# Row sums of ten attention heads with one more addition and half the columns, in a score buffer

## The chip, the cores and the metric

The program runs on one core of a Trainium2 chip. The metric is the time of one execution on the device, in microseconds (us). The engines are TensorE (PE in the rows, its weight loads PEld), VectorE (DVE), ScalarE (ACT), GpSimd (POOL) and SyncE (SP, which issues DMAs).

## What is computed

Clustered attention over 2 x 8 heads of 768 tokens with 64 dimensions, then a mixture of experts with a capacity of 384 rows. The change touches the row sums of the softmax alone (`np.sum(attn, ...)`).

```python
mask = q_assign[:, :, :, None] == k_assign[:, :, None, :]
scores = np.where(mask, scale * np.matmul(q, k.transpose(0, 1, 3, 2)), -1000000000.0)
attn = np.exp(scores - np.max(scores, axis=-1, keepdims=True))
attn = attn / (np.sum(attn, axis=-1, keepdims=True) + 1e-09)
attn_out = np.matmul(attn, v)
...
logits = x @ w_gate                     # x: attn_out, one row a token
h = np.maximum(np.einsum('ecd,edf->ecf', disp, w1), 0.0)
y = np.einsum('ecf,efd->ecd', h, w2)
out[i] = gate_w[i] * y[expert_idx[i], pos[i]]
```

## The kernel before

The 16 heads run one after the other. I call the stretch in which head i's scores are made stage i; the stages take the first 250 us, the experts the rest. On PE, DVE, ACT and POOL the order of the instructions is that in which the code is written, so an instruction that waits holds all behind it on its engine.

Stage i has twelve steps g = 0 to 11 (`st_group`, L401): two matmuls make a 128 x 384 tile of transposed scores in a PSUM buffer `s` (pool `psS`, three buffers that rotate), and ACT writes its exponential to `pf`. Six such tiles (three key tiles, two query halves) make one half u of a head, `pt[h, u]`. Behind each step stands `ahead` (L1255): one maximum of a later head, a matmul into a buffer `m` (pool `psM`, two buffers) and a DVE reduction `mx` of it; a matmul into a buffer must wait until the reduction of two maxima earlier is done. At the steps in `TWICE` (L57) two are made, which brings the chain of maxima ahead of the heads. When a head's twelve maxima are done, DVE joins them (`max_chain`, tile `mxx`), and two steps later `max_rows` (L381) turns them on PE (`mtp`) and sends them by ACT and a DMA to the operand that the head's second score matmul reads.

`hooks` (L708) puts the other work between the steps. At g = 2 of stage i: the second half of head i - 1's product with v (`pv_batch`, tile `o`), `out_scale(i - 2)` on DVE (tiles `lt`, `lg`, `x`), `p_add(i - 1, 1)` on DVE, and `sum_strips(i - 1)` on PE (tile `rsp`); in some even stages then `cl_strips` (tile `ccp`), also in strips; on ACT the copies `rs` and `oT`; on POOL the subtractions `ql` of `split` for head i + 3. At g = 5 and 6 the sums are turned on PE (`rtp`) and inverted on DVE (`r`). At g = 8: the first half of head i's product with v, `p_add(i, 0)`, and POOL's subtractions `Y` for a later head.

`sum_strips` (L440) adds over the 128 partitions by matmuls with a block of ones, 32 columns of weights each, so that four of them stand side by side in the array, a strip of 32 output partitions each. Strips 0 and 1 read `acc` (the sum of key tiles 0 and 1 that `p_add` made) for the two query halves, strips 2 and 3 the third key tile from `pf`. The two halves u accumulate in the same strips. `sum_scale` adds strip 0 to 2 and strip 1 to 3. The sums stand in pool `psT`, two buffers that are shared with `ctb`, `ccp`, `ctp`, `mtp` and `otp`.

Head 15 has sums of its own (`last_batch`), and head 0's are made ahead of stage 1. Stages 10 and 12 also have the gating of the first 768 tokens on DVE, stages 12 to 15 splits of the first expert weights (`w_split`, tile `ws`).

Of the kernel before, what the change touches and what calls it, by code (L numbers as in the profile page):

```python
# [7 lines left out]
F32 = mybir.dt.float32  # L8
# [4 lines left out]
ALU = mybir.AluOpType  # L13
# [3 lines left out]
P = 128  # L17
# [6 lines left out]
def kernel(  # L24
# [13 lines left out]
    nc = tc.nc  # L38
# [5 lines left out]
    HALF = S // 2  # L44
# [9 lines left out]
    WARM1 = 1  # L54
    WARM2 = 2
    G_B0, G_B1, G_TURN, G_OUT = 8, 2, 5, 11
    TWICE = {(1, 1), (1, 2), (2, 2), (2, 3), (3, 2), (4, 2)}  # L57
    HELD = (mybir.EngineType.PE, mybir.EngineType.DVE, mybir.EngineType.Activation, mybir.EngineType.Pool)
    G1B = range(8)
    W_AT = [(12, 8), (13, 2), (13, 8), (14, 2), (14, 8), (15, 2), (15, 6)]  # L60
# [11 lines left out]
    psS = ctx.enter_context(tc.tile_pool(name="psS", bufs=3, space=PSUM))  # L72
    psM = ctx.enter_context(tc.tile_pool(name="psM", bufs=2, space=PSUM))
    psO = ctx.enter_context(tc.tile_pool(name="psO", bufs=1, space=PSUM))
    psT = ctx.enter_context(tc.tile_pool(name="psT", bufs=2, space=PSUM))
# [51 lines left out]
    def keep(ins):  # L127
        if held[0] and ins.ins.engine in HELD:
            tc.keep_in_program_order(ins)
# [36 lines left out]
    def load_v(pi):  # L166
        b, hp = divmod(pi, NP)
        t = work.tile([P, 2, NT, D], F32, tag="v", name="v", bufs=2)
        nc.sync.dma_start(out=t, in_=v1[b, hp])
        vt[pi] = t  # L170
# [221 lines left out]
    pt = {}  # L392
    ot = {}
    oT_t = {}
    acc = {}
# [21 lines left out]
    def p_add(h, u):  # L417
        a = acc[h, u] = work.tile([P, 2, HALF], F32, tag="acc", name="acc", bufs=3)
        keep(nc.vector.tensor_tensor(out=a, in0=pt[h, u][:, 0], in1=pt[h, u][:, 1], op=ALU.add))

    def pv_batch(h, u, ns=range(TH)):
        if (u, ns[0]) == (0, 0):
            ot[h] = psO.tile([P, 512], F32, tag="o", name="o")
        pf = pt[h, u]
        for n in ns:
            kt = u * TH + n
            for j in range(2):
                keep(nc.tensor.matmul(  # L428
                    out=ot[h][j * D:(j + 1) * D, 0:HALF],
                    lhsT=vt[h // 2][:, h % 2, kt, :],  # L430
                    rhs=pf[:, n, j],
                    start=(kt == 0),
                    stop=(kt == NT - 1),
                ))
# [3 lines left out]
        keep(nc.scalar.activation(out=oT_t[h], in_=ot.pop(h)[:, 0:HALF], func=AF.Copy))  # L438

    def sum_strips(h):  # L440
        ps = psT.tile([P, 512], F32, tag="t", name="rsp")
        for u in range(2):
            parts = acc.pop((h, u)), pt.pop((h, u))[:, 2]
            for q in range(4):
                keep(nc.tensor.matmul(
                    out=ps[32 * q:32 * q + 32, 0:HALF],
                    lhsT=onef[:, 0:32],
                    rhs=parts[q // 2][:, q % 2],
                    start=(u == 0),
                    stop=(u == 1),  # L450
                ))
        rt_t[h] = ps

# [103 lines left out]
    def out_scale(h):  # L557
        b, hh = divmod(h, H)
        tv = oT_t.pop(h)[:, 0:NT * OW].rearrange("p (c j o) -> p j c o", c=TH, j=2)
        r = rt_t.pop(h).rearrange("p j (c o) -> p j c o", o=1)  # L560

        def by_half(x):
            return x.rearrange("p (j c) e -> p j c e", j=2)

        lg = by_half(xt[b, "l"])
        if hh == 0:
            keep(nc.vector.tensor_tensor(out=lg, in0=tv[:, :, :, D:OW], in1=r.to_broadcast([P, 2, TH, E]), op=ALU.mult))
        else:
            lt = work.tile([P, 2, TH, E], F32, tag="lt", name="lt")
            keep(nc.vector.tensor_tensor(out=lt, in0=tv[:, :, :, D:OW], in1=r.to_broadcast([P, 2, TH, E]), op=ALU.mult))  # L570
            keep(nc.vector.tensor_tensor(out=lg, in0=lg, in1=lt, op=ALU.add))
        keep(nc.vector.tensor_tensor(
            out=by_half(xt[b][:, :, hh * D:(hh + 1) * D]),
            in0=tv[:, :, :, 0:D],
            in1=r.to_broadcast([P, 2, TH, D]),
            op=ALU.mult,
        ))
# [130 lines left out]
    def hooks(i, g):  # L708
        even, pi = i % 2 == 0, i // 2
        if g == (0 if i % 2 else 5) and 2 <= i < 2 + E:  # L710
            zero_fill(i - 2)
        if (i, g) == (NH - 2, 0):
            sta.close()
            wslot.append(ctx.enter_context(tc.tile_pool(name="wsl", bufs=1, reuse_waits="tile")))
            for c in range(NA, NW):
                slots.append(wslot[0].tile([P, 2, 1024], R32, name=f"ws{c}"))
        if g == 5 and i in (H + 2, H + 3):
            for c in range(2):
                w_load(2 * (i - H - 2) + c)
        if (i, g) == (H + 4, 5):  # L720
            close_tile()
        if (i, g) == (H + 5, 6):
            row0.append(wra.tile([P, XR], F32, tag="z", name="row0", bufs=1))
            nc.sync.dma_start(out=row0[0], in_=xd[0:P, :])
        if not even and g == 0 and pi + 3 < NH // 2:
            load_pair(pi + 3)
        if even and g == 4 and i > 0 and pi + 1 < NH // 2:
            load_v(pi + 1)

        if i == 1 and g == 4 or not even and 1 < i < NH - 3 and g == 1:  # L730
            p = 2 if i == 1 else (i + 3) // 2
            cl_turn(p)
            gens["c"] = cl_assign(p, nc.gpsimd)
        if i == 1 and g in (5, 6):
            next(gens["c"])
        if even and i > 0 and pi + 1 < NH // 2 and g == 0:
            cl_back(pi + 1)

        if i > 0 and g == G_TURN:
            sum_turn(i - 1)  # L740
        if i > 0 and g == G_TURN + 1:
            sum_scale(i - 1)
        if i > 0 and g == (6 if i == NH - 1 else G_OUT):
            out_stage(i - 1)
        if (i, g) in W_AT:
            w_high(W_AT.index((i, g)))
        if g == G_B1 and i > 0:
            if i > 1:
                pv_batch(i - 1, 1)
            if i > 1:  # L750
                out_scale(i - 2)
            if i > 1:
                p_add(i - 1, 1)
                sum_strips(i - 1)
            if strips_at(i):
                cl_strips(strips_at(i))
            if i + 3 < NH:
                split(i + 3, 0)
            if not even and 1 < i < NH - 3:
                next(gens["c"])  # L760
                next(gens["c"])
            if i == H + 2:
                gens["g"] = gate(0)
                next(gens["g"])
                next(gens["g"])
            if i == H + 4:
                for _ in gens["g"]:
                    pass
            if i > 1:
                sum_evict(i - 1)  # L770
                pv_evict(i - 1)
            if strips_at(i):
                cl_evict(strips_at(i))
        if g == G_B0 and i < NH - 1:
            pv_batch(i, 0)
            p_add(i, 0)
            if 0 < i < NH - 3:
                split(i + 3, 1)
                split(i + 3, 2)
            if i == H + 2:  # L780
                next(gens["g"])
            if not even and i < NH - 3:
                for _ in gens["c"]:
                    pass
        if g == G_B0 + 1 and 0 < i < NH - 3:
            split(i + 3, 3)
        if (i, g) in W_AT:
            c = W_AT.index((i, g))
            w_split(c)
            w_load(c + NA)  # L790
        if (i, g) == (NH - 2, G_B0):
            for nm in ("qv", "kv"):
                xa.append(work.tile([P, S], R32, tag=nm, name="xa", bufs=2)[:, 0:DM].rearrange("p (k n) -> p k n", n=P))
            turn(row0[0][:, 0:DM], *xa, psT, "t")
        if i == NH - 1:
            if g == 5:
                keep(nc.vector.tensor_tensor(out=rhl, in0=rhb[:, H - 1, 0:OW], in1=rhb[:, H - 1, OW:2 * OW], op=ALU.add))
                p_add(i, 0)
            if g == 6:
                last_batch(i, 0)  # L800
                sum_evict(i)
                pv_evict(i)
            if g == 7:
                out_scale(i - 1)
            if g == 8:
                sum_turn(i)
            if g == 9:
                last_rows(i, 0)
            if g == 10:
                p_add(i, 1)  # L810
                last_logits(i, 0)
                gens["g"] = gate(B - 1, 0, TH)
                next(gens["g"])
            if g == 11:
                next(gens["g"])
                last_scale(i, 0)
# [448 lines left out]
    with ExitStack():  # L1265
# [3 lines left out]
        for i in range(1, NH):  # L1269
            if i < H + 2:  # L1270
                tc.no_sync_barrier()
            for g in range(2 * NT):
                st_group(i, g)
                ahead(1 + ((i, g) in TWICE), 2 * NT * i + g)
                if 2 * NT * i + g in rows_at:
                    max_rows(rows_at[2 * NT * i + g])
                hooks(i, g)
        h = NH - 1
# [89 lines left out]
```

## Time and profile before

| | |
|---|---|
| Time before | 456.97 us, median of 3 runs (455.88 to 457.72) |
| The profiled execution | 454.88 us |
| Its span, from the first to the last instruction | 453.1 us |
| Granted TensorE clock, mean | 0.998 of full speed |
| Busy share of the span | PE 96%, PEld 75%, DVE 71%, ACT 61%, POOL 31% |
| Stages 1 to 15 | 35.4 to 250.4 us of the span |

The rows below are of one execution, the profiled one, so a sum that is made from them is made against its 454.88 us. Matmuls overlap in the rows: a matmul of 384 columns is shown with some 0.34 or 0.49 us, while the next starts after 0.18 or 0.32 us. What one costs is read from start to start.

### The profile page before, as it was taken

To read this page: it belongs to the slowest core of one execution; us is meant where nothing else is said; L and a number is where in the kernel's file an instruction comes from. 1 tells how busy PE (TensorE), PEld (TensorE's weight loads), DVE (VectorE), ACT (ScalarE), POOL (GpSimd) and SP (SyncE) were. 2 spreads that over 40 slices of the span, in tenths; PEclk is the share of its full clock that TensorE was granted. 3 is DMA by queue.
4 is the path that set the end of the run, shared out by engine and by line. 5 is a ranking of instruction groups with operands and counts; after the bars stand their busy time and mean duration, and the time that the engine had idled before them with its cause. 6 is when DMAs were issued, how large, how long until landed. Compare 5 with 4: busy or idle time off the path is not lost. (4 is left out here: it accounts for less than half of the span.)

```text
span 453.1 us, 8094 instructions
## 1 busy us (share of the span) xinstructions
PE 437.1 (96%) x2806; PEld 341.8 (75%) x2806; DVE 321.7 (71%) x676; ACT 274.7 (61%) x548; POOL 139.4 (31%) x173
## 2 busy tenths in 40 slices
PE   8899999999999999999999999999999999999983
PEld 8766576666756676675765577999999999999962
DVE  5996678678586788888865645778777778786411
ACT  4766565656656575566665335668786868686330
POOL 7864635363644634354100220001010101001010
PEclk9999999999999999999999999999999999999999
DMA  8455474482763964128322165669787787876010
GB/s 278 108 139 159 130 219 134 111 295 44 206 214 91 309 237 102 37 50 262 116 94 93 73 223 180 212 222 288 243 256 259 242 263 229 281 229 197 14 39 18
DMA packets 31222, 78.13 MB, mean 172 GB/s; under 512 B 4678, under 2 KB 5024, under 8 KB 31172
## 3 DMA queue, kind: packets, MB, share of 16 engines
q1 hardware_dynamic: 26196, 61.18, 44.8%
q0 software_dynamic: 4832, 16.15, 9.5%
q8 instruction: 29, 0.48, 0.4%
q14 instruction: 21, 0.17, 0.1%
q10 hardware_dynamic: 144, 0.16, 0.1%
HBM read 50.46 MB, written 16.76 MB: 148 GB/s over the span
## 5 line engine op out<-in xcount | busy, mean ns | idle before, releaser
L353 DVE TENSOR_REDUCE mx<-m 128x1 f32<-128x384 f32 x192 | 102.5, 553 | 41.9 <-PE m L346 38.6
L413 ACT ACTIVATE pf<-s 128x384 f32<-128x384 f32 x192 | 90.8, 492 | 45.7 <-PE s L409 39.2
L139 DVE TENSOR_TENSOR ws<-wraw,ws 128x1024 fp32r<-128x1024 f32 x64 | 78.3, 1223 | 25.8 <-ACT ws L133 25.4
L408 PE MATMUL s<-W,Y 112*128 112x384 f32 (+1 forms) x192 | 73.2, 381 | 0.1
L948 PE MATMUL g<-xc,ws 128*128 128x416 f32 x224 | 70.0, 373 | 1.1 <-PEq L1088 0.2
L948 PE MATMUL g<-hc,ws 128*128 128x416 f32 x224 | 69.5, 371 | 0.0
L675 POOL DMA_INDIRECT out_dram<-y,row x17 | 17.9, 1054 | 166.7 <-ACT pt L956 75.8
L346 PE MATMUL m<-Y,W 112*128 112x384 f32 (+1 forms) x192 | 66.5, 354 | 1.9 <-DVE mx L353 1.1
L133 ACT ACTIVATE ws<-wraw 128x1024 fp32r<-128x1024 f32 x64 | 67.1, 1049 | 0.3 <-issue 0.2
L409 PE MATMUL s<-Qs,Y 97*128 97x384 f32 (+1 forms) x192 | 65.1, 339 | 0.2 <-DMA Qs<-mr 0.2
L428 PE MATMUL o<-pf,v 128*64 128x384 f32 x360 | 64.7, 494 | 0.5 <-DVE r L470 0.5
L949 PE MATMUL g<-xc,ws 128*128 128x208 f32 x224 | 58.0, 259 | 0.0
L949 PE MATMUL g<-hc,ws 128*128 128x208 f32 x224 | 57.9, 259 | 0.0
L308 POOL TENSOR_TENSOR Y<-kv,Y 64x256 fp32r<-64x256 f32 x48 | 41.5, 890 | 45.9 <-ACT Y L327 39.9
L308 POOL TENSOR_TENSOR ql<-qv,W 64x256 fp32r<-64x256 f32 x45 | 40.7, 928 | 46.5 <-issue 24.6
L408 PEld LDWEIGHTS s<-W,Y 112*128 112x128 f32 (+1 forms) x192 | 36.2, 189 | 19.6 <-issue 16.6
L956 ACT ACTIVATE pt<-g 128x208 f32<-128x208 f32 x84 | 27.4, 339 | 30.7 <-PE g L949 30.5
L428 PEld LDWEIGHTS o<-pf,v 128*64 128x64 f32 x360 | 23.3, 136 | 28.2 <-issue 24.4
L948 PEld LDWEIGHTS g<-xc,ws 128*128 128x128 f32 x224 | 42.1, 188 | 3.2 <-issue 2.8
L949 PEld LDWEIGHTS g<-xc,ws 128*128 128x128 f32 x224 | 42.8, 191 | 0.0
L949 PEld LDWEIGHTS g<-hc,ws 128*128 128x128 f32 x224 | 42.8, 191 | 0.0
L948 PEld LDWEIGHTS g<-hc,ws 128*128 128x128 f32 x224 | 42.1, 188 | 0.4
(204 smaller groups left out, 680.9 us busy)
## 6 DMA issues: line engine op xcount, KB each, us to landing
wraw<-in_w_dram SPq DMA_DIRECT2D x64, 512.0 KB
xd<-z POOLq DMA_DIRECT2D x7, 780.0 KB
row<-xd SPq DMA_DIRECT2D x18, 260.0 KB
qv<-in_qT_dram SPq DMA_DIRECT2D x8, 384.0 KB
kv<-in_kT_dram SPq DMA_DIRECT2D x8, 384.0 KB
v<-in_v_dram SPq DMA_DIRECT2D x8, 384.0 KB
Y<-Y SPq DMA_DIRECT2D x32, 96.0 KB
Qs<-W SPq DMA_DIRECT2D x16, 192.0 KB
```

The costliest lines, as they stand in the source:

```text
L133: keep(nc.scalar.activation(out=w[:, 0], in_=raw[c], func=AF.Copy))
L139: keep(nc.vector.tensor_tensor(out=w[:, 1], in0=t, in1=w[:, 0].bitcast(F32), op=ALU.subtract))
L308: keep(eng.tensor_tensor(out=out[:, cc], in0=a[:, cc], in1=b[:, cc].bitcast(F32), op=ALU.subtract))
L346: keep(nc.tensor.matmul(out=m[:, 0:HALF], lhsT=W[0:KA[h % 2], t * P:(t + 1) * P], rhs=Y1[0:KA[h % 2], j * HALF:(j + 1) * HALF], start=True ...
L353: keep(nc.vector.tensor_reduce(out=mxt[h][:, j, t:t + 1], in_=m[:, 0:HALF], axis=AX.X, op=ALU.max))
L408: keep(nc.tensor.matmul(out=s[:, 0:HALF], lhsT=Y1[0:ka, ks], rhs=W[0:ka, qs], start=True, stop=False))
L409: keep(nc.tensor.matmul(out=s[:, 0:HALF], lhsT=Y0[0:kb, ks], rhs=Qs[0:kb, qs], start=False, stop=True))
L413: keep(nc.scalar.activation(out=pt[h, u][:, slot[0], slot[1]], in_=s[:, 0:HALF], func=AF.Exp, scale=1.0 / float(D) ** 0.5))
L428: keep(nc.tensor.matmul(out=ot[h][j * D:(j + 1) * D, 0:HALF], lhsT=vt[h // 2][:, h % 2, kt, :], rhs=pf[:, n, j], start=(kt == 0), stop=(kt ...
L948: nc.tensor.matmul(out=o, lhsT=w[0], rhs=x.rearrange("p o n -> p (o n)"), start=start, stop=False)
L949: nc.tensor.matmul(out=o[:, 0:RW], lhsT=w[1], rhs=x[:, 0], start=False, stop=stop)
L956: nc.scalar.activation(out=t, in_=o[:, RW:2 * RW], func=AF.Copy)
```

## The change

- For ten heads (`THREE`) DVE adds the third key tile to `acc` of the first half, u = 0 (`p_add_rest`). For even heads this stands right behind `p_add(i, 0)` at g = 8 of their own stage; for odd heads behind `p_add(i - 1, 1)` at g = 2 of the next stage. Both are even stages: 2, 4, 6, 8 and 14.
- In these heads `sum_strips` takes u = 1 first, as before over 384 columns in each strip. Then u = 0 has one operand for each query half, and its four strips take 192 columns each: strips 0 and 1 the first 192, strips 2 and 3 the last 192. `sum_scale` still adds strip 0 to 2 and 1 to 3.
- All sums but head 0's stand in a buffer of `psS`.
- At g = 2 `p_add(i - 1, 1)` now stands ahead of `out_scale(i - 2)` on DVE, in all stages.
- `TWICE` loses (2, 2), (2, 3) and (4, 2) and gets (3, 3): four extra maxima where there were six.

```diff
--- before.py
+++ after.py
@@ -54,7 +54,8 @@
     WARM1 = 1
     WARM2 = 2
     G_B0, G_B1, G_TURN, G_OUT = 8, 2, 5, 11
-    TWICE = {(1, 1), (1, 2), (2, 2), (2, 3), (3, 2), (4, 2)}
+    TWICE = {(1, 1), (1, 2), (3, 2), (3, 3)}
+    THREE = (1, 2, 3, 4, 5, 6, 7, 8, 13, 14)
     HELD = (mybir.EngineType.PE, mybir.EngineType.DVE, mybir.EngineType.Activation, mybir.EngineType.Pool)
     G1B = range(8)
     W_AT = [(12, 8), (13, 2), (13, 8), (14, 2), (14, 8), (15, 2), (15, 6)]
@@ -418,6 +419,10 @@
         a = acc[h, u] = work.tile([P, 2, HALF], F32, tag="acc", name="acc", bufs=3)
         keep(nc.vector.tensor_tensor(out=a, in0=pt[h, u][:, 0], in1=pt[h, u][:, 1], op=ALU.add))
 
+    def p_add_rest(h):
+        a = acc[h, 0]
+        keep(nc.vector.tensor_tensor(out=a, in0=a, in1=pt[h, 0][:, 2], op=ALU.add))
+
     def pv_batch(h, u, ns=range(TH)):
         if (u, ns[0]) == (0, 0):
             ot[h] = psO.tile([P, 512], F32, tag="o", name="o")
@@ -438,16 +443,20 @@
         keep(nc.scalar.activation(out=oT_t[h], in_=ot.pop(h)[:, 0:HALF], func=AF.Copy))
 
     def sum_strips(h):
-        ps = psT.tile([P, 512], F32, tag="t", name="rsp")
-        for u in range(2):
-            parts = acc.pop((h, u)), pt.pop((h, u))[:, 2]
+        ps = psS.tile([P, 512], F32, tag="s", name="rsp") if h else psT.tile([P, 512], F32, tag="t", name="rsp")
+        short = h in THREE
+        for u in (1, 0) if short else (0, 1):
+            a, p2 = acc.pop((h, u)), pt.pop((h, u))[:, 2]
             for q in range(4):
+                cs_ = slice(0, HALF)
+                if short and u == 0:
+                    cs_ = slice(q // 2 * (HALF // 2), (q // 2 + 1) * (HALF // 2))
                 keep(nc.tensor.matmul(
-                    out=ps[32 * q:32 * q + 32, 0:HALF],
+                    out=ps[32 * q:32 * q + 32, cs_],
                     lhsT=onef[:, 0:32],
-                    rhs=parts[q // 2][:, q % 2],
-                    start=(u == 0),
-                    stop=(u == 1),
+                    rhs=(a if q < 2 or cs_.stop - cs_.start < HALF else p2)[:, q % 2, cs_],
+                    start=(u == int(short)),
+                    stop=(u != int(short)),
                 ))
         rt_t[h] = ps
 
@@ -748,9 +757,10 @@
             if i > 1:
                 pv_batch(i - 1, 1)
             if i > 1:
+                p_add(i - 1, 1)
+                if even and i - 1 in THREE:
+                    p_add_rest(i - 1)
                 out_scale(i - 2)
-            if i > 1:
-                p_add(i - 1, 1)
                 sum_strips(i - 1)
             if strips_at(i):
                 cl_strips(strips_at(i))
@@ -774,6 +784,8 @@
         if g == G_B0 and i < NH - 1:
             pv_batch(i, 0)
             p_add(i, 0)
+            if even and i in THREE:
+                p_add_rest(i)
             if 0 < i < NH - 3:
                 split(i + 3, 1)
                 split(i + 3, 2)
```

DVE at g = 2 of an even stage, here stage 6, before (`mx`: maxima; `mxx`: `max_chain`; `lt`, `lg`, `x`: `out_scale(4)`; the `acc` row: `p_add(5, 1)`; the rows `r`: `sum_scale(5)`; the last row: `p_add(6, 0)`):

```order
L353 TENSOR_REDUCE mx<-m 128x1 x6
L359 TENSOR_TENSOR mxx<-mx 128x6
L570 TENSOR_TENSOR lt<-otp,r 128x48
L571 TENSOR_TENSOR lg<-lg,lt 128x48
L572 TENSOR_TENSOR x<-otp,r 128x6x64
L419 TENSOR_TENSOR acc<-pf 128x768
L353 TENSOR_REDUCE mx<-m 128x1 x4
L469 TENSOR_SCALAR r_1538<-rtp 128x6
L470 TENSOR_TENSOR r<-rtp,r_1538 128x6
L471 RECIPROCAL r<-r 128x6
L353 TENSOR_REDUCE mx<-m 128x1 x2
L419 TENSOR_TENSOR acc<-pf 128x768
```

The same place now, up to the `mxx`, which has moved from behind the step g = 2 to behind g = 4 (L420 is `p_add`, L424 `p_add_rest`):

```order
L354 TENSOR_REDUCE mx<-m 128x1 x6
L420 TENSOR_TENSOR acc<-pf 128x768
L424 TENSOR_TENSOR acc<-acc,pf 128x768
L579 TENSOR_TENSOR lt<-otp,r 128x48
L580 TENSOR_TENSOR lg<-lg,lt 128x48
L581 TENSOR_TENSOR x<-otp,r 128x6x64
L354 TENSOR_REDUCE mx<-m 128x1 x2
L360 TENSOR_TENSOR mxx<-mx 128x6
```

`out_scale` stands behind two additions, and `p_add` ahead of it by three instructions.

PE at g = 2 of stage 6, before: the product with v, the sums of head 5 with u = 0 and then u = 1, `cl_strips`, and the step g = 3.

```order
L428 MATMUL o<-pf,v 64x384 x6
L445 MATMUL rsp<-acc,onef 32x384 x2
L445 MATMUL rsp<-pf,onef 32x384 x2
L445 MATMUL rsp<-acc,onef 32x384 x2
L445 MATMUL rsp<-pf,onef 32x384 x2
L194 MATMUL ccp<-qv,cbs 32x384
L194 MATMUL ccp<-kv,cbs 32x384
```

And now, where the first two rows of sums are u = 1 and the third is u = 0:

```order
L433 MATMUL o<-pf,v 64x384 x6
L454 MATMUL rsp<-acc,onef 32x384 x2
L454 MATMUL rsp<-pf,onef 32x384 x2
L454 MATMUL rsp<-acc,onef 32x192 x4
L195 MATMUL ccp<-qv,cbs 32x384
L195 MATMUL ccp<-kv,cbs 32x384
```

Four matmuls of 384 columns have become four of 192, and all four read `acc`.

DVE in stage 14, where the last maxima are made, before: from g = 0 to the addition at g = 8 (`ws`: `w_split` at g = 2).

```order
L353 TENSOR_REDUCE mx<-m 128x1 x6
L359 TENSOR_TENSOR mxx<-mx 128x6
L570 TENSOR_TENSOR lt<-otp,r 128x48
L571 TENSOR_TENSOR lg<-lg,lt 128x48
L572 TENSOR_TENSOR x<-otp,r 128x6x64
L419 TENSOR_TENSOR acc<-pf 128x768
L139 TENSOR_TENSOR ws_117<-wraw,ws_117 128x1024
L469 TENSOR_SCALAR r_2951<-rtp 128x6
```

And now, from the additions of g = 2 to those of g = 8:

```order
L420 TENSOR_TENSOR acc<-pf 128x768
L424 TENSOR_TENSOR acc<-acc,pf 128x768
L579 TENSOR_TENSOR lt<-otp,r 128x48
L580 TENSOR_TENSOR lg<-lg,lt 128x48
L581 TENSOR_TENSOR x<-otp,r 128x6x64
L140 TENSOR_TENSOR ws_117<-wraw,ws_117 128x1024
L354 TENSOR_REDUCE mx<-m 128x1 x2
L360 TENSOR_TENSOR mxx<-mx 128x6
L478 TENSOR_SCALAR r_2960<-rtp 128x6
L479 TENSOR_TENSOR r<-rtp,r_2960 128x6
L480 RECIPROCAL r<-r 128x6
L420 TENSOR_TENSOR acc<-pf 128x768
```

Two maxima and `mxx` have moved behind the `ws` of 1024 columns, and `mtp` on PE, which reads `mxx`, from behind g = 4 to behind g = 6.

## Rows read from the trace of the kernel before

**Rows 1.** The page, part 1: busy us, share of the span, instructions.

```profile
PE 437.1 (96%) x2806; PEld 341.8 (75%) x2806; DVE 321.7 (71%) x676; ACT 274.7 (61%) x548; POOL 139.4 (31%) x173
```

**Rows 2.** Busy by stretch: PE, PEld, DVE, ACT, POOL; granted clock, DMA share, GB/s.

```profile
94.28:108.44 14.16, 14.13 (x92) 9.37 (x91) 11.91 (x26) 8.08 (x17) 7.50 (x9) 1.00 0.58 191
108.44:123.09 14.65, 14.65 (x104) 9.73 (x102) 9.50 (x22) 9.60 (x19) 7.25 (x9) 1.00 0.53 149
...
223.98:236.49 12.51, 12.51 (x84) 7.97 (x83) 8.00 (x16) 8.15 (x18) 0.00 (x0) 1.00 0.26 88
255.00:440.00 185.00, 181.90 (x1176) 171.13 (x1174) 126.93 (x242) 118.82 (x240) 22.46 (x22) 1.00 0.66 211
```

**Rows 3.** Waits of ScalarE: who waited for whom, us, times, longest.

```profile
ACT pf L413 <- PE s L409: 39.2, 45, 2.1
```

**Rows 4.** Timeline of PE, stage 6, step 2: start, us, instruction.

```profile
112.70 0.52 PE L445 MATMUL rsp<-acc,onef 128*32 128x384 f32 x2
...
113.37 0.49 PE L445 MATMUL rsp<-acc,onef 128*32 128x384 f32 x2
...
114.01 0.49 PE L194 MATMUL ccp<-qv,cbs 128*32 128x384 f32 x1
```

**Rows 5.** Timeline of PE in stage 14, steps 4 to 6.

```profile
230.12 0.27 PE L386 MATMUL mtp<-cs,mxx 128*6 128x128 f32 x1
...
230.59 0.49 PE L463 MATMUL rtp<-cs,rs 128*128 128x128 f32 x3
230.84 0.42 PE L408 MATMUL s<-W,Y 112*128 112x384 f32 x1
```

**Rows 6.** Timeline of PE, then of DVE, stage 5, step 2.

```profile
98.49 0.52 PE L445 MATMUL rsp<-acc,onef 128*32 128x384 f32 x2
...
98.83 0.49 PE L445 MATMUL rsp<-acc,onef 128*32 128x384 f32 x2
...
99.37 0.52 PE L445 MATMUL rsp<-acc,onef 128*32 128x384 f32 x2
...
97.18 0.20 DVE L570 TENSOR_TENSOR lt<-otp,r 128x48 f32<-128x48 f32 x1
...
98.01 1.31 DVE L419 TENSOR_TENSOR acc<-pf 128x768 f32<-128x768 f32 x1
```

**Rows 7.** Timeline of DVE and POOL, stage 6, step 2.

```profile
111.31 0.17 DVE L359 TENSOR_TENSOR mxx<-mx 128x6 f32<-128x6 f32 x1
...
112.22 0.95 DVE L419 TENSOR_TENSOR acc<-pf 128x768 f32<-128x768 f32 x1
...
112.36 2.79 POOL L308 TENSOR_TENSOR ql<-qv,W 64x256 fp32r<-64x256 f32 x3 [4.20 <-issue]
```

**Rows 8.** Timeline of DVE and POOL before stage 1, two additions in a row.

```profile
30.39 0.94 DVE L419 TENSOR_TENSOR acc<-pf 128x768 f32<-128x768 f32 x1
...
31.26 1.49 DVE L419 TENSOR_TENSOR acc<-pf 128x768 f32<-128x768 f32 x1
...
30.41 1.53 POOL L308 TENSOR_TENSOR ql<-qv,W 64x256 fp32r<-64x256 f32 x1
```

**Rows 9.** Timeline of DVE, POOL and PE, stage 6, from step 8.

```profile
119.52 0.95 DVE L419 TENSOR_TENSOR acc<-pf 128x768 f32<-128x768 f32 x1
121.55 0.56 DVE L353 TENSOR_REDUCE mx<-m 128x1 f32<-128x384 f32 x1 [1.09 <-PE m L346]
...
119.96 1.09 POOL L308 TENSOR_TENSOR Y<-kv,Y 64x256 fp32r<-64x256 f32 x1 [3.49 <-ACT Y L327]
...
122.23 0.38 PE L346 MATMUL m<-Y,W 112*128 112x384 f32 x1
```

**Rows 10.** Timeline of DVE, stage 14, step 2.

```profile
228.27 1.22 DVE L139 TENSOR_TENSOR ws<-wraw,ws 128x1024 fp32r<-128x1024 f32 x1
```

**Rows 11.** Timeline of PE, stage 2, behind the second doubled maximum.

```profile
56.90 0.34 PE L409 MATMUL s<-Qs,Y 97*128 97x384 f32 x1
57.36 0.45 PE L346 MATMUL m<-Y,W 128*128 128x384 f32 x1
```

## The prediction

> **What bounds the kernel now.** I read the busy shares first. PE is busy 96% of the span [rows 1], but its rows overlap, so I looked at stages by themselves: PE is covered in all of them at full clock (14.13 of 14.16 us in stage 5, 14.65 of 14.65 in stage 6, 12.51 of 12.51 in stage 14), and in the experts 181.9 of 185 us [rows 2]. ACT waits for PE (39.2 us for the score matmuls alone [rows 3]), not PE for ACT. In PE's timeline the starts follow each other at a fixed pace with few gaps. So PE's pace sets the time: columns that PE no longer streams come off the end one to one, and what else changes costs only where PE then has to wait. Since the experts are held by PE too, what the stages gain is not taken back there.
>
> DVE is busy 11.91 of 14.16 us in the odd stage 5, 9.50 of 14.65 us in the even stage 6 and 8.00 of 12.51 us in stage 14 [rows 2]. All ten new additions lie in even stages, two in each of 2, 4, 6, 8 and 14. At 0.95 us each [rows 7] stage 6 would hold 11.4 us, less than the odd stages hold now. By the sum DVE has room; the question is where in the stage the additions stand.
>
> **The change part by part.**
>
> *Columns.* In stage 6 the sum with u = 1 starts at 113.37 and what follows it, in strips too, at 114.01 [rows 4]: two steps of 0.32 us over 384 columns, four strips side by side in each. With 192 columns I take half, 0.16 us a step. A transpose of 128 columns takes 0.11 us (three of them and the start of the next matmul in 0.25 us, the last one overlapped [rows 5]), which lies on the same line, columns in proportion. Ten heads, two steps: 10 x 2 x 0.16 = 3.2 us less. The bounds: 0 if a step doesn't shrink at all, 4.2 us if it falls to the 0.11 us of the transposes.
>
> *Order on DVE at g = 2.* In stage 5 the sum starts at 98.49, its second step at 98.83, and u = 1 at 99.37 instead of about 99.15: PE waits some 0.2 us for `p_add`, which starts at 98.01 behind `out_scale` and runs until 99.32 [rows 6]. Stages 7, 9 and 11 show the same gap; together 0.7 us. Now `p_add` takes the place of `lt`, at 97.18, and ends near 98.13, ahead of 98.49, when PE wants it. That holds for u = 1 first too. I take 0.7 us less; the bounds are 0 and 0.8.
>
> *The added addition of odd heads, g = 2 of stages 2, 4, 6, 8, 14.* In stage 6 `p_add` moves up to where `mxx` stood, 111.31 [rows 7], and ends at about 112.25; the second addition follows, until 113.2. PE wants u = 1 at 112.70 and u = 0 two steps later, at 113.37 [rows 4]. Cost 0, with 0.15 us to spare. The cover is the 0.64 us of u = 1. `out_scale` ends 0.95 us later, about 114.1. Behind it on DVE stand only maxima, the next of which PE makes after 114.8, and `mtp`, which now has `otp`'s buffer, two steps behind. The bound: POOL's `ql` starts at 112.36 [rows 7], and the wait below shows that an addition that starts behind it loses 0.55 us. In four stages that is 2.2 us (stage 14 has no work on POOL [rows 2]).
>
> *The added addition of even heads, g = 8.* `p_add(6, 0)` runs from 119.52 to 120.47, and POOL's `Y` starts inside it, at 119.96, and takes 1.09 us [rows 9]. The second addition reads what the first has written. What two additions and POOL do to each other is seen before stage 1: the first takes 0.94 us, the second 1.49, while POOL's piece beside them takes 1.53 [rows 8]. They exclude each other, and POOL gets in between. So the second ends at 121.05 (the end of POOL's piece) + 0.82 = 121.87, not at 121.42. The next maximum started at 121.55 [rows 9] and now starts near 121.8; PE's matmul of 122.23 needs its buffer, so it waits about 0.16 us. Stage 8 gives the same, stage 4 also, stage 2 some 0.1 us: 0.6 us more in all. Stage 14 has no maxima left there. The bounds are 0 and 4 x 0.55 = 2.2 us, if all of the loss reaches PE.
>
> The page "SBUF — State Buffer" of the Trainium skill, section "Who interferes with whom", says the same as a rule: an addition with both inputs in SBUF and a GpSimd instruction that reads SBUF lock each other out, and whoever issues first keeps the ports for its whole instruction. It speaks against the change, since the change puts ten such additions beside POOL's subtractions; without the rule the second addition of g = 8 would end at 121.42, before the maximum of 121.55, and the sum would be -3.6 us instead of -3.0. The trace agrees with the rule (1.49 us against 0.94 [rows 8]).
>
> *The sums in a score buffer.* A sum takes a `psS` buffer from behind g = 2 until ACT has copied it. Steps 3 and 4 have the two others, whose exponentials are done during the product with v, and step 5 comes later than the copy. Cost 0, since PE arrives at step 5 over 1.5 us after the sum; the bound is a rival below. In `psT` the four other users keep two buffers; I find no wait there that ends later than now.
>
> *Fewer extra maxima.* The matmuls are the same in number. Behind the second doubled maximum of stage 2 PE waits 0.28 us (a start-to-start time of 0.46 us, 56.90 to 57.36 [rows 11], instead of 0.18), and that goes. The new double at (3, 3) stands behind DVE's longest string in a stage (an addition, `out_scale`, two instructions of the assignment), and I charge it the same 0.28 us. Sum 0, between a loss of 0.4 and a gain of 0.4 us. `max_rows` comes two steps later from stage 3 on; six steps remain until its row is read.
>
> *Stage 14.* Two maxima now fall behind g = 2, and DVE makes them behind the second addition, `out_scale` and `ws` (1.22 us [rows 10]). `ws` ended at 229.49; with 0.95 us of addition it ends at 230.3, since `mxx` no longer stands ahead. Two maxima and `mxx` bring it to 231.5. PE comes to `mtp` behind g = 6, at about 231.3 (step 6 began at 230.84 [rows 5] and takes 0.45 us; the sums are 0.32 us shorter, two maxima of 0.18 us come in), and holds the rest of stage 14 behind it. I take 0.3 us more, between 0 and 1.2 (the whole `ws`).
>
> **The sum**: -3.2 - 0.7 + 0 + 0.6 + 0 + 0 + 0.3 = -3.0 us. The profiled execution would take 454.88 - 3.0 = 451.9 us. It lies 2.1 us below the median of the runs shown and 1.0 us below the lowest of them, so I carry only the difference over to the median: 456.97 - 3.0 = 454.0 us, 0.7% faster. About 0.5%, 2.3 us, is what a measurement of this kernel can tell from no change.
>
> **The rivals.**
>
> *A. POOL gets in between the additions at g = 2 too.* For it: the margin in stage 6 is about 0.15 us for `ql` against the start of the second addition, at 112.2, and 0.15 us for PE. Against it: the addition is ready first and needs nothing from the one ahead of it. Price: 4 x 0.55 = 2.2 us, so 456.2 us, no change that can be told. The rule of the Trainium skill's page "SBUF — State Buffer" that is told above is this mechanism; the trace agrees with it there, and shows nothing of who comes first here.
>
> *B. The change doesn't do what it says: a step doesn't get shorter with its columns.* Four weight loads stand before each step. If these set the 0.32 us, the 3.2 us are not there, and 0.2 us is lost: 457.2 us. Against it: the transposes' 0.11 us [rows 5].
>
> *C. Slower: the sum holds up the scores.* If step 5, or a step before, has to wait for the buffer of the sum, one exponential's length of 0.49 us is lost in each of the 14 stages that keep a sum there: 6.9 us, so 460.9 us. It decides from 5.3 us on, 0.38 us a stage. Against it: ACT waits for PE, and not the other way [rows 3], and two of three buffers are free when PE comes out of the product with v.
>
> **How the numbers follow.** The forecast has a chance of 0.71, A 0.12, B 0.09, C 0.08. The forecast alone reaches from 4.8 us less (no loss at g = 8 and in stage 14, 0.8 for the order, 0.4 for the maxima, and 0.4 more for the columns, at 0.14 us a step) to 1.9 us less (0.8 more lost at g = 8, 0.3 more in stage 14): 452.2 to 455.1 us. To leave out no more than 2 in 10 the range takes in A as well: 452.2 to 456.2 us. Faster by over 0.5%: 0.71; within 0.5% (A and B): 0.21; slower (C): 0.08.
>
> **What would show it.** Right: the second half of the sums in two steps of 0.16 us in ten heads; no gap inside the sums of stages 5, 7, 9 and 11; the even stages 6 and 8 some 0.15 us shorter and odd ones 0.3 (3 and 15) to 0.5 (5, 7 and 9); second additions of about 1.4 us at g = 8 and 0.95 at g = 2; a short wait for `mtp` in stage 14. Wrong: PE waiting for an addition ahead of u = 0, steps of the halved sums over 0.2 us, score matmuls that wait for ACT behind a sum, or maxima late behind g = 8 by more than 0.3 us.

## The result, and the profile after

The changed kernel takes 450.16 us (median of six runs, 448.91 to 452.88) against 456.5 us for the kernel before, run beside it (454.41 to 457.72). The ratio is 0.988, with an interval of 0.985 to 0.992, which is 5.3 us less (3.8 to 6.8); by the two medians it is 6.3. Run again later, the same pair gave 451.22 against 455.88 us, 0.990 (0.987 to 0.993). I had forecast 454.0 us in a range of 452.2 to 456.2: the direction was right, the size was not.

The page of the changed kernel, part 1, as in [rows 1], for its profiled execution (448.91 us, span 447.1 us):

```profile
PE 432.0 (97%) x2806; PEld 342.1 (77%) x2806; DVE 330.4 (74%) x686; ACT 275.4 (62%) x548; POOL 137.9 (31%) x173
```

PE is still the engine that sets the pace: it has 5.1 us less to do than in [rows 1], and the span is 6.0 us shorter. DVE has ten instructions and 8.7 us more; the waits that this makes for PE cost some 0.8 us, as told below. By stretch (columns as in [rows 2]), stages 2 to 6, stage 14 and a part of the experts:

```profile
48.61:63.27 14.66, 14.64 (x103) 9.88 (x102) 11.30 (x23) 9.62 (x19) 7.61 (x9) 1.00 0.58 173
63.27:77.62 14.35, 14.23 (x95) 9.79 (x93) 12.72 (x28) 8.27 (x17) 7.67 (x9) 1.00 0.59 189
77.62:92.07 14.45, 14.45 (x103) 9.69 (x102) 11.72 (x24) 9.57 (x19) 7.16 (x9) 1.00 0.55 159
92.07:105.66 13.59, 13.59 (x92) 9.45 (x91) 11.75 (x26) 8.14 (x17) 7.21 (x9) 1.00 0.60 198
105.66:120.14 14.48, 14.48 (x104) 9.68 (x102) 11.74 (x24) 9.59 (x19) 7.19 (x9) 1.00 0.55 153
218.26:230.80 12.54, 12.54 (x86) 8.35 (x85) 10.83 (x21) 8.31 (x18) 0.00 (x0) 1.00 0.27 86
249.00:434.00 185.00, 181.82 (x1176) 171.06 (x1174) 126.97 (x242) 118.82 (x240) 22.43 (x22) 1.00 0.68 211
```

Stage 5 fell from 14.16 to 13.59 us, stage 6 from 14.65 to 14.48, stage 14 is as long as it was, and the experts too [rows 2]. For stages 2 to 4 the kernel before, in a second profile of it, stands here:

```profile
50.79:66.52 15.73, 15.47 (x106) 9.90 (x104) 10.81 (x23) 9.60 (x19) 7.44 (x9) 1.00 0.54 162
66.52:80.78 14.26, 14.26 (x94) 9.60 (x92) 11.96 (x27) 8.16 (x17) 7.42 (x9) 1.00 0.62 190
80.78:96.04 15.26, 15.13 (x105) 9.82 (x103) 10.23 (x23) 9.62 (x19) 7.28 (x9) 1.00 0.51 149
```

The two largest gains of a stage, 1.07 us in stage 2 and 0.81 in stage 4, are where I had expected little. They are the stages that lose doubled maxima, two in stage 2 and one in stage 4.

### The profile page after: what moved, and what is told of

It reads as the page before. It is cut to its first block, busy times and chain, and to the rows that moved or that the text cites. A ratio compares the mean times of both kernels' runs of the same rounds, so it can differ in the third digit from the quotient of the medians.

```text
span 447.1 us, 8102 instructions
## 1 busy us (share of the span) xinstructions
PE 432.0 (97%) x2806; PEld 342.1 (77%) x2806; DVE 330.4 (74%) x686; ACT 275.4 (62%) x548; POOL 137.9 (31%) x173
## 5 line engine op out<-in xcount | busy, mean ns | idle before, releaser
L309 POOL TENSOR_TENSOR Y<-kv,Y 64x256 fp32r<-64x256 f32 x48 | 43.5, 930 | 43.0 <-ACT Y L328 37.9
L309 POOL TENSOR_TENSOR ql<-qv,W 64x256 fp32r<-64x256 f32 x45 | 35.9, 822 | 44.9 <-issue 24.9
```

What stands on the lines that cost most here:

```text
L309: keep(eng.tensor_tensor(out=out[:, cc], in0=a[:, cc], in1=b[:, cc].bitcast(F32), op=ALU.subtract))
```

## The experiments

Single runs of this kernel scatter by up to 4 us, as far as the profiles show by what lies ahead of stage 1 and by single stalls (last section). So besides each ratio to the kernel before on the same chip I compare stages: a stage runs from its head's first score matmul to the next head's (stage 15 to the end of its last one), and one in which nothing is changed repeats within 0.05 us, but for the stalls told below, stage 12 of the first profile of before (0.19 us longer than in e1) and stage 1 of e8. What lies behind stage 15 takes 202.7 us in before, e1, after and e9 alike. The base is the second profile of before, e1; the sum is that of stages 1 to 15.

| run | median us | ratio to before (interval) | sum of stages 1 to 15, us |
|---|---|---|---|
| e1 before again | 454.55 | 0.9995 (0.9985 to 1.0005) | 213.71 |
| e2 maxima alone | 453.74 | 0.998 (0.997 to 0.999) | 212.84 |
| e3 order alone | 459.03 | 1.009 (1.007 to 1.011) | 217.33 |
| e4 full columns | 452.40 | 0.995 (0.994 to 0.997) | 211.83 |
| e5 old maxima | 453.13 | 0.995 (0.993 to 0.997) | 212.26, with a stall |
| e6 sums in psT | 457.22 | 1.003 (1.001 to 1.004) | 216.87, with a stall |
| e7 rest later | 454.23 | 0.997 (0.995 to 0.999) | 212.09, with a stall |
| e8 two doubles | 453.14 | 0.995 (0.993 to 0.997) | 211.98, with a stall |
| e9 after again | 451.22 | 0.990 (0.987 to 0.993) | 209.44 |
| e10 twelve heads | 452.06 | 0.992 (0.988 to 0.995) | 209.66 |
| e11 a double at (5, 2) | 451.43 | 0.991 (0.988 to 0.995) | 209.13 |
| e12 both | 449.80 | 0.988 (0.984 to 0.991) | 209.05 |

The first profile of after has 209.37. The stall is one of 1.0 to 2.2 us in stage 12, told in the last section; where a cost is given for e5 to e8, stage 12 is left out.

### The kernel before, again

No edit.

> The kernel before, unchanged, profiled once more. Theory 1: of the 6.0 us by which the profiled span got shorter, about 1.0 us is a single stall in stage 13 of the kernel before (stage 13 took 14.64 us, 13.59 after) and 0.4 us an earlier start of stage 0, both of them chance of that one execution. Then stage 13 takes 13.6 to 13.7 us here and the time is that of before, ratio 1.000. Rival: the stall belongs to the kernel before and the change took it away; then stage 13 takes 14.6 us again.

The profile of before that the prediction went by holds a stall in stage 13 (14.64 us) that this one doesn't have (13.60). So of the 6.0 us between the first two profiles 1.0 us was never the change's; in all, stages 1 to 15 of that first profile are 1.29 us longer than those of e1. From e1 to after, stages 1 to 15 lose 4.34 us, and that is the size to explain.

### The maxima alone

```diff
-    TWICE = {(1, 1), (1, 2), (2, 2), (2, 3), (3, 2), (4, 2)}
+    TWICE = {(1, 1), (1, 2), (3, 2), (3, 3)}
```

> Before with the new list of doubled maxima alone. Theory 1, from the two traces: a second maximum at (2, 2), (2, 3) and (4, 2) costs PE 0.55 to 0.58 us each, of which 0.18 us is its own matmul, the new one at (3, 3) costs 0.56 us, and a maximum that falls into stage 14 costs 0.18 us; stages 2, 3, 4 and 14 together get 0.8 us shorter, ratio about 0.998. The prediction's theory: 0, stages together within 0.2 us.

Its stages 2, 3 and 4:

```profile
48.43:63.18 14.75, 14.75 (x103) 9.89 (x102) 9.30 (x21) 9.65 (x19) 7.07 (x9) 1.00 0.58 172
63.18:77.87 14.69, 14.56 (x94) 9.70 (x93) 12.52 (x28) 8.22 (x17) 7.41 (x9) 1.00 0.59 184
77.87:92.52 14.65, 14.65 (x103) 9.69 (x102) 9.41 (x22) 9.57 (x19) 6.99 (x10) 1.00 0.53 155
```

Stage 2 loses 0.98 us, stage 4 0.61, stage 3 gains 0.43 and stage 14 0.18: 0.98 us less in the four, 0.87 in all stages, where my sum had 0. The wait that I had missed stands in the kernel before at the ends of the steps g = 2. Its timelines of PE in stages 2 and 4 and of DVE beside them:

```profile
50.91 0.90 PE L346 MATMUL m<-Y,W 128*128 128x384 f32 x2
51.74 2.16 PE L428 MATMUL o<-pf,v 128*64 128x384 f32 x12
...
80.93 0.90 PE L346 MATMUL m<-Y,W 128*128 128x384 f32 x2
81.76 1.19 PE L428 MATMUL o<-pf,v 128*64 128x384 f32 x6
...
50.76 1.65 DVE L353 TENSOR_REDUCE mx<-m 128x1 f32<-128x384 f32 x3 [0.38 <-PE m L346]
```

the weight load of the second maximum in stage 2, from a timeline of PEld:

```profile
51.37 0.19 PEld L346 LDWEIGHTS m<-Y,W 128*128 128x128 f32 x1 [0.44 <-DVE mx L353]
```

and the same place of stage 4 after:

```profile
79.52 0.33 PE L347 MATMUL m<-Y,W 128*128 128x384 f32 x1
79.78 1.19 PE L433 MATMUL o<-pf,v 128*64 128x384 f32 x6
```

From the first maximum to the product with v it is 0.83 us with two maxima and 0.26 with one. The second costs 0.57 us, not the 0.18 of a matmul: with two `m` buffers it waits for the reduction of the maximum two before it, which DVE starts at 50.76. It starts 0.46 us behind the first instead of 0.18, and the product behind it 0.37 us later instead of 0.26. The joined row of PE doesn't say so. It joins the two matmuls into one busy time of 0.90 us, and two of 384 columns show 0.52 us where nothing waits.

### The order alone

```diff
             if i > 1:
-                out_scale(i - 2)
-            if i > 1:
                 p_add(i - 1, 1)
+                out_scale(i - 2)
                 sum_strips(i - 1)
```

> Before with p_add ahead of out_scale at g = 2, nothing else; the sums stay in psT. Theory 1: the sums of stages 5, 7, 9 and 11 lose their 0.2 us gap, 0.9 us less, ratio about 0.998. Rival: out_scale, now 0.95 us later, frees otp's buffer later, which the next tile in psT waits for (the sums in odd stages, ccp in even ones); then the gap comes back ahead of the sums, and the time is that of before or up to 3 us more, ratio 1.000 to 1.007.

Slower: the odd stages 3 to 11 take 0.7 to 0.9 us more each, 3.6 us in the sum. Timelines of DVE and PE, stage 5:

```profile
99.60 0.95 DVE L419 TENSOR_TENSOR acc<-pf 128x768 f32<-128x768 f32 x1
...
101.13 0.55 DVE L572 TENSOR_TENSOR x<-otp,r 128x384 f32<-128x384 f32 x1
...
101.82 0.52 PE L445 MATMUL rsp<-acc,onef 128*32 128x384 f32 x2 [0.84 <-DVE x L572]
```

The addition is done early, as wanted, and the gap inside the sum is gone (its first three steps start at 101.82, 102.14 and 102.46 us), but the whole sum now waits for `x`. In `psT` the buffer that it gets is that of `otp`, which `out_scale` reads, and `out_scale` is now the later one.

### The changed kernel with full columns

```diff
-    THREE = (1, 2, 3, 4, 5, 6, 7, 8, 13, 14)
+    THREE = ()
```

> The changed kernel with no head in THREE: no third addition, all sums over 384 columns in both halves; doubled maxima, order on DVE and the score buffer as changed. Theory 1: 20 steps of 0.16 us come back (3.2 us) and the waits behind g = 8 of stages 2, 4, 6 and 8 go (0.6 us): 2.6 us more than the changed kernel, so ratio to before about 0.994 to 0.996. Rival: the columns are not what the change is about and most comes from the buffer and the order; then the ratio stays near 0.988.

Against e2, with the order and the score buffer together, stages 5, 7, 9 and 11 lose 0.22 to 0.24 us each and no other over 0.04: 1.01 us in the sum. From here to after, the columns and the third additions bring 2.46 us: 0.32 to 0.34 us in stages 3, 5, 7, 9 and 15, and 0.09 to 0.22 in 2, 4, 6, 8 and 14.

### The changed kernel with the old maxima

```diff
-    TWICE = {(1, 1), (1, 2), (3, 2), (3, 3)}
+    TWICE = {(1, 1), (1, 2), (2, 2), (2, 3), (3, 2), (4, 2)}
```

> The changed kernel with the old six doubled maxima. Theory 1: stages 2, 3, 4 and 14 together get 0.8 us longer than in the changed kernel, because each doubled maximum ahead of a product with v or behind a sum makes PE wait 0.38 us for DVE beside its own 0.18 us. The prediction's theory: no difference.

The old list costs 1.9 us in the changed kernel, twice as much as in the kernel before: stage 2 is 1.15 us longer, stage 4 1.14. There is a second price. Timelines of DVE, POOL and PE in stage 4:

```profile
83.27 0.95 DVE L420 TENSOR_TENSOR acc<-pf 128x768 f32<-128x768 f32 x1
84.14 1.50 DVE L424 TENSOR_TENSOR acc<-acc,pf 128x768 f32<-128x768 f32 x1
...
83.67 3.25 POOL L309 TENSOR_TENSOR ql<-qv,W 64x256 fp32r<-64x256 f32 x3 [4.20 <-issue]
...
84.92 0.49 PE L454 MATMUL rsp<-acc,onef 128*32 128x384 f32 x2
...
85.69 0.53 PE L454 MATMUL rsp<-acc,onef 128*32 128x192 f32 x8 [0.26 <-DVE acc L424]
```

With two maxima at the end of the step the additions come later against POOL, whose `ql` is issued 0.47 us ahead of the second one (in stage 4 of after it is 0.31 us behind it, 81.54 against 81.23 us). The second addition takes 1.50 us, and the halved sums start 0.77 us behind the last step of the whole ones instead of 0.32. This is my rival A, and it comes true as soon as the additions are late.

### The changed kernel with all sums in psT

```diff
-        ps = psS.tile([P, 512], F32, tag="s", name="rsp") if h else psT.tile([P, 512], F32, tag="t", name="rsp")
+        ps = psT.tile([P, 512], F32, tag="t", name="rsp")
```

> The changed kernel with the sums back in psT. Theory 1: the sums of odd stages then stand in the buffer that out_scale frees, and ccp in even ones; out_scale now ends behind one or two additions, 0.45 to 0.56 us after PE wants the buffer. Ten or eleven stages lose some 0.5 us: 4 to 5.5 us more than the changed kernel, ratio to before 0.998 to 1.001. Rival (the prediction's, which priced the buffer at nothing): psT has room, no difference to the changed kernel.

The stages are 5.4 us longer than after: 0.7 to 1.0 in the odd ones from 3 to 11, 0.5 in 4, 6 and 8. The waits of PE, whole span: who waited, for whom, us, times, longest.

```profile
PE rsp L454 <- DVE x L581: 3.4, 5, 0.9
...
PE ccp L195 <- DVE x L581: 0.9, 3, 0.3
```

The buffer, which I had priced at nothing, is the condition of the new order.

### The second addition of even heads a step later

```diff
         if g == G_B0 and i < NH - 1:
             pv_batch(i, 0)
             p_add(i, 0)
-            if even and i in THREE:
-                p_add_rest(i)
...
+        if g == G_B0 + 1 and even and i in THREE:
+            p_add_rest(i)
```

> The changed kernel with the third addition of even heads one step later, behind the maximum of g = 9. Theory 1: the waits of PE behind g = 8 in stages 2, 4, 6 and 8, some 0.15 us each, go, since the maximum of g = 9 no longer stands behind two additions and POOL: 0.5 us less than the changed kernel. Rival: the addition meets POOL's next subtraction, takes 1.3 us again and holds up the maxima of g = 10 and 11; then the first steps of the next stage wait, no gain.

Stages 2, 4, 6 and 8 are 0.12 to 0.23 us shorter and 3, 5, 7 and 9 0.26 to 0.39 longer, 0.55 us more in all. DVE behind g = 9 of stage 6:

```profile
119.59 0.56 DVE L354 TENSOR_REDUCE mx<-m 128x1 f32<-128x384 f32 x1 [1.17 <-PE m L347]
120.07 1.17 DVE L424 TENSOR_TENSOR acc<-acc,pf 128x768 f32<-128x768 f32 x1
```

DVE had been idle for 1.17 us ahead of this place. The addition would have fitted there, and now holds up the last maxima of the stage: PE's first maximum of stage 7 starts 0.37 us behind the score matmul ahead of it instead of 0.18. The rival was right.

### The changed kernel with two doubles

```diff
-    TWICE = {(1, 1), (1, 2), (3, 2), (3, 3)}
+    TWICE = {(1, 1), (1, 2)}
```

> The changed kernel with doubled maxima at (1, 1) and (1, 2) alone. Theory 1: stage 3 loses the 0.6 us of its doubles beyond the two matmuls that move to stage 14, 0.4 us less in all; the rows of the maxima come two steps later still, at g = 8 with four steps to spare. Rival: the row's turning then stands at g = 8 ahead of the product with v in every stage and waits for DVE, or the row lands late; then stages 4 to 14 get longer by 0.1 us or more each and the time goes up by 1 us or more.

Stage 3 loses 0.61 us, but each of stages 4 to 9 is 0.12 to 0.20 longer and stage 14, which now makes more maxima, 0.90: some 1.3 us more. Stage 1 is 0.31 us shorter, but not by the change: in after its second score matmul waits for the DMA of `Qs`, here it doesn't, and stage 0 is 0.31 us longer; without it the two doubles cost 1.6 us. `mtp` now stands at g = 8, right ahead of the product with v, as the rival had it. That its place there is what costs in stages 4 to 9 is inferred; no run moves it alone. Two doubles are too few here.

### The changed kernel again, and three ways on

```diff
# e10
-    THREE = (1, 2, 3, 4, 5, 6, 7, 8, 13, 14)
+    THREE = (1, 2, 3, 4, 5, 6, 7, 8, 9, 11, 13, 14)
# e11
-    TWICE = {(1, 1), (1, 2), (3, 2), (3, 3)}
+    TWICE = {(1, 1), (1, 2), (3, 2), (5, 2)}
# e12: TWICE as e11, and
+    THREE = (1, 2, 3, 4, 5, 6, 7, 8, 11, 13, 14)
```

> The changed kernel, unchanged, profiled and timed once more. The stages that the change reaches got 4.4 us shorter from trace to trace when single stalls (stage 0, 12 or 13) and the start are left out. Theory 1: the time follows that, ratio 0.989 to 0.992 (4.1 to 5.0 us). Rival: the 6.0 us between the two first profiles are the change; then the ratio is 0.987 or less. The prediction's 3.0 us would be 0.9934.

> The changed kernel with heads 9 and 11 in THREE too, whose third additions fall to g = 2 of stages 10 and 12, ahead of the gating on DVE. Theory 1: stage 12 has room (DVE was idle 1.1 us ahead of the next maximum) and gets 0.3 us shorter; in stage 10 DVE was idle 0.6 us only, so the addition of 0.95 us makes the maxima of g = 3 and 4 late and PE waits 0.2 to 0.4 us: stage 10 as long as before or longer by 0.1. Rival: DVE's share of the span decides (74%), both get 0.3 us shorter.

> The changed kernel with the doubled maximum of (3, 3) moved to (5, 2). At (3, 2) a double costs PE 0.23 us in the trace, its own 0.18 us included, at (3, 3) 0.56 us. Theory 1: place decides, 0.3 us less in stages 3 to 5 together. Rival: a double costs the same wait wherever DVE has p_add behind it, no difference.

> The changed kernel with head 11 in THREE too and the double of (3, 3) at (5, 2). If both parts hold: 0.6 us less than the changed kernel, ratio to it 0.9987, the shortest of all versions; stage 12 0.3 us shorter, stages 3 to 5 0.3 us shorter.

e9 repeats the stages of after within 0.04 us, and its ratio lies where Theory 1 had it. e10 finds no room: stage 10 is 0.06 us longer, 12 shorter by 0.05, 13 longer by 0.25. DVE has the gating in stages 10 and 12, and behind it a weight load of PE waits for a maximum's reduction, 0.5 us in stage 10 and 0.4 in stage 12, where none waits in e9; in stage 13 that of `mtp` waits 0.3 us for `mxx`. Of the 0.64 us of columns nothing is left, in stage 12 against my expectation. e11 moves the double from (3, 3) to (5, 2): stage 3 falls by 0.52 us and stage 5 rises by 0.24, 0.28 less. The stall of (3, 3) in after is the one I had charged; PE in stage 3:

```profile
69.80 0.34 PE L410 MATMUL s<-Qs,Y 128*128 128x384 f32 x1
70.26 0.44 PE L347 MATMUL m<-Y,W 112*128 112x384 f32 x1
```

0.46 us from start to start instead of 0.18. e12 has both stages at 13.82, with PE covered throughout:

```profile
64.57:78.39 13.82, 13.82 (x93) 9.64 (x92) 12.30 (x27) 8.15 (x17) 7.67 (x9) 1.00 0.59 194
92.84:106.66 13.82, 13.82 (x94) 9.64 (x92) 12.21 (x27) 8.13 (x17) 7.68 (x9) 1.00 0.58 196
```

Head 11 adds only 0.05 us. With 449.80 us e12 has the lowest median of all runs, but the times alone don't tell it from e9 (the intervals overlap); its stages are 0.3 to 0.4 us shorter than those of after and e9, where I had expected 0.6.

## Why the prediction was wrong

| term of the sum | forecast, us | measured in the stages, us |
|---|---|---|
| fewer extra maxima | 0 | -0.87 |
| order, with the score buffer | -0.7 | -1.01 |
| columns, with what the second additions cost at g = 8 and in stage 14 | -2.3 | -2.46 |
| sum | -3.0 | -4.34 |

**The step that failed is "Fewer extra maxima ... Sum 0".** I had looked for the stall in one place, behind (2, 3), where a row of its own shows it [rows 11]. At (2, 2) and (4, 2) PE waits as well, 0.39 us each beyond the matmul's 0.18 (0.57 - 0.18), at the end of a joined row. The price at (3, 3) was right: a stall of 0.28. So the change takes three stalls away and makes one, and I had cancelled one against one. I had also left out that the matmul behind a stalled one comes some 0.1 us late as well (57.64 behind 57.36 us in before, 70.53 behind 70.26 in after, 0.28 and 0.27 us instead of 0.18); the 0.39 us hold that. The -0.87 us lie outside the bounds that I had given this term, a loss or a gain of 0.4, and are most of the 1.34 us by which the stages beat my sum. The two maxima that come to stage 14 in exchange cost 0.18 us there.

**Order.** The mechanism was right. PE and DVE at g = 2 of stage 5 now, against [rows 6]:

```profile
96.26 0.52 PE L454 MATMUL rsp<-acc,onef 128*32 128x384 f32 x2
...
96.61 0.49 PE L454 MATMUL rsp<-acc,onef 128*32 128x384 f32 x2
...
96.93 0.51 PE L454 MATMUL rsp<-acc,onef 128*32 128x192 f32 x8
97.37 0.45 PE L409 MATMUL s<-W,Y 128*128 128x384 f32 x1
...
94.76 0.95 DVE L420 TENSOR_TENSOR acc<-pf 128x768 f32<-128x768 f32 x1
```

No gap is left inside the sums, and each of the four odd stages gave back 0.23 us where I had taken 0.7 us for all of them; my own reading of stage 5, 0.22 us four times, would have made 0.9. What I got wrong beside it is where the gain comes from. I called the buffer a cost of 0 and found no wait in `psT`; e3 shows that the order without the buffer loses 3.6 us, and e6 that the whole change without it loses 5.4 us against after. What the buffer would do without the order no run shows.

**Columns.** Right: in stage 6 the halved strips take 0.32 us for two steps, where each step took 0.32 [rows 4]. Timelines of PE and DVE, g = 2:

```profile
110.27 0.49 PE L454 MATMUL rsp<-acc,onef 128*32 128x384 f32 x2
...
110.59 0.51 PE L454 MATMUL rsp<-acc,onef 128*32 128x192 f32 x8
110.91 0.49 PE L195 MATMUL ccp<-qv,cbs 128*32 128x384 f32 x1
...
109.28 0.95 DVE L424 TENSOR_TENSOR acc<-acc,pf 128x768 f32<-128x768 f32 x1
110.15 0.20 DVE L579 TENSOR_TENSOR lt<-otp,r 128x48 f32<-128x48 f32 x1
```

The second addition is done by 110.15, 0.44 us ahead of the halved strips where I had 0.15: two additions in a row take 1.73 us from their start at 108.42, not twice 0.95, and the first starts 0.1 us earlier against PE. POOL's `ql` is issued only at 109.58, 0.30 us behind the second addition's start, and there it is POOL's piece that gets longer (1.25 us, the next two 0.73 and 0.74). Rival A thus had more against it in this kernel than I saw, though e5 shows it at work, and rival B fell with the 0.16 us a step. Rival C didn't come true: no score matmul waits for a sum's buffer.

**The second addition at g = 8.** DVE, then PE, in stage 6 after, against [rows 9]:

```profile
116.34 0.95 DVE L420 TENSOR_TENSOR acc<-pf 128x768 f32<-128x768 f32 x1
117.39 1.30 DVE L424 TENSOR_TENSOR acc<-acc,pf 128x768 f32<-128x768 f32 x1
...
118.95 0.33 PE L410 MATMUL s<-Qs,Y 97*128 97x384 f32 x1
119.21 0.45 PE L347 MATMUL m<-Y,W 112*128 112x384 f32 x1
```

It takes 1.30 us where I had 1.4, with POOL's `Y` beside it, and PE's `m` comes 0.26 us behind the score matmul instead of 0.18, `otp` behind it 0.29 us later instead of 0.22. Stages 2, 4, 6 and 8 give back 0.10 to 0.23 us of the 0.32 from the columns, 0.6 in all, as forecast. In part that is luck: in stage 6 the wait is half of the 0.16 us that I had, and the other half is the late start behind it, which I hadn't priced. In stage 14, where POOL has nothing to do (so eight of the ten additions stand beside POOL, not all ten), the two additions of g = 8 take 0.92 and 0.96 us:

```profile
225.98 0.92 DVE L420 TENSOR_TENSOR acc<-pf 128x768 f32<-128x768 f32 x1
227.00 0.96 DVE L424 TENSOR_TENSOR acc<-acc,pf 128x768 f32<-128x768 f32 x1
```

The Trainium skill's page "SBUF — State Buffer", section "Who interferes with whom", has additions of this kind and GpSimd's reads exclude each other. The three lengths of the same addition agree with it: 0.96 us with POOL idle, 1.30 and 1.50 us where POOL's piece was issued first. In both of these the addition ends 0.82 us behind the end of POOL's piece (118.69 behind 117.88 us; in e5 85.63 behind 84.82).

**Stage 14.** `mtp` starts 0.33 us behind the score matmul ahead of it (225.29 and 225.62), a wait of some 0.15 us where I had 0.3.

**What the sum doesn't hold.** The stages explain 4.3 us. The median of the first comparison fell by 6.3 us, of the second by 4.7; the 4.3 us lie inside the intervals of both (3.8 to 6.8 and 3.1 to 6.1). My range was made from the bounds of the terms, and nothing in it stood for runs of one kernel that lie 3 to 4 us apart, though the three times shown already spread over 1.8 us. A forecast of -4.3 us would have given 452.6 us, inside the range; the measured median lies 2.5 us below even that. Behind stage 15 the profiles of before and after don't differ, so I put the rest down to what lies ahead of stage 1 and to single stalls (last section). How much of it each timed run had isn't shown, and that part stays open.

## What to carry to other kernels

A row that joins several instructions hides the waits between them: take the time from start to start, at every place where the pattern stands, before charging one stall against another. When two instructions change places on an engine, look at which buffers the earlier one used to free; the order here pays only together with another buffer for the sum. Where single runs scatter as much as the change is worth, compare the stages and profile the old kernel twice.

## What the runs showed of the hardware

**A stall of PE's signals.** In the first profile of before, stage 13, the semaphore updates of PE's matmuls stop at 209.47 us for 1.6 us and then come 34 to 43 ns apart, as if they had been held back. The others wait meanwhile. Waits of 209 to 212 us:

```profile
ACT pf L413 <- PE s L409: 1.6, 2, 1.3
DVE mx L353 <- PE s L409: 1.4, 2, 1.2
...
PE m L346 <- DVE mx L353: 0.8, 1, 0.8
```

The four runs e5 to e8, of one chip, have it in stage 12 (1.0 to 2.2 us). In all five it lies near the last two of POOL's six scatter transfers of the first 768 tokens; the other profiles have these transfers at the same place and no stall. I don't know what holds the updates back. Nor is it known which of the timed runs had the stall: the ratio of e7 fits with it, that of e5 and e6 without.

**The clock in stage 0.** The twelve runs of e1 lie at 454.4 to 454.6 us, nine of them, and at 455.5 to 455.6. The three longer ones have a mean granted clock of 0.994, the nine others 0.996 to 0.998. The profiled one is of the longer group, and its stage 0 takes 16.71 us instead of 15.34. Windows of it from 14 us on (columns as in [rows 2]):

```profile
14.00:20.46 6.46, 5.29 (x39) 4.18 (x37) 6.13 (x13) 5.16 (x7) 6.38 (x9) 1.00 0.20 47
20.46:24.00 3.54, 3.23 (x16) 2.91 (x14) 2.90 (x8) 1.87 (x4) 3.35 (x6) 0.71 0.51 117
24.00:28.00 4.00, 4.00 (x21) 3.54 (x19) 2.91 (x6) 3.00 (x7) 2.50 (x4) 0.83 0.93 281
```

A granted clock of 0.71 and 0.83 is a part of the stretch at 1.2 GHz and the rest at 2.4. PE was covered for 82% of the stretch ahead of it (5.29 of 6.46 us), and for 79% (4.48 of 5.66 us) in that of after, where the clock stayed at 1.00. The profile of e3 has the same fall (0.67 and 0.88, a stage 0 of 16.72 us), that of e9 none, with PE covered for 87% of the stretch ahead (6.06 of 6.96 us). So these rows don't tell what let it fall.

**The start.** Stage 0 begins at 19.4 to 23.7 us of the span in these profiles; e9 and after, the same kernel, differ by 3.3 us there. The times of the profiled runs go with it: after, with stage 0 at 19.7 us, took 448.91 us, the shortest of its six runs, and e10, with 23.7, took 453.56 us, the longest of its six. Besides the stalls and the 0.19 us of stage 12, what differs between profiles of one kernel lies ahead of stage 1.
